# Ten instead of eight dummy products ahead of the first turn of the keys

## The chip, the cores and the metric

One core of one Trainium2 chip. The metric is the device time of one execution in microseconds (us), as a median over runs; lower is better. A profile gives the span of one execution; the device time of the same execution is 1.7 us longer (258.93 us for the profiled one of the kernel before, with a span of 257.2 us).

## The reference

Attention over 4 batches, 8 heads, 768 positions of 64, with a band of 16 positions and 24 block summaries, followed by a gated feed-forward layer on 3072 tokens of 512:

```python
k_sum = k.reshape(B, H, nb, block, D).max(axis=3)
v_sum = v.reshape(B, H, nb, block, D).mean(axis=3)
# scores on the band and on the block maxima, one softmax over both, then
x = attention_output                               # 3072 x 512
g = x @ w_gate; val = x @ w_val
ffn_out = gelu(g) * val @ w_out
return x + sigmoid(x @ w_res) * ffn_out
```

## The kernel before

The kernel works in eight units of 384 tokens. The parts that count here are its head, in which the first keys and queries are turned (transposed by TensorE), and the order in which weights are loaded. A "dummy" is a product of a tile of zeros with itself, whose result nobody reads.

```python
def keep_warm(n, wp=None):
    ...
    for i in range(n):
        nc.tensor.matmul(wp[:], warm[:, 0:128], warm[:], start=True, stop=True)

# loads on GpSimd's queue, in this order: keys, queries, values of the first unit (the keys and
# queries of its first two heads go on SyncE's queue), then
for c in range(6):
    sl = slice(c * 256, (c + 1) * 256)
    if c == 5:
        load_tokens(qb, q, 0, TU, S, 0, H)
    nc.gpsimd.dma_start(out=w_gate[:, :, sl], in_=wg_src[:, :, sl])
    nc.gpsimd.dma_start(out=w_val[:, :, sl], in_=wv_src[:, :, sl])
nc.gpsimd.dma_start(out=w_res[:], ...)
# ... w_out in three parts, then the next batch

# the head of TensorE's program
s1 = s_tiles((AO, TT))
keep_warm(8, s1[0])
nc.scalar.copy(kt[:, 0]..., kf[:, 0])              # cast of the first keys
nc.vector.tensor_copy(kt[:, 1]..., kf[:, 1])
nc.vector.tensor_copy(qa[:, 0:2]..., qf[:])
t = k_first(0)                                     # first turn of keys, 16 products
q_step(qa, 0, 0, TU, 0, *MM, nc.vector.tensor_copy)
keep_warm(2, s1[0])
# ... second turn, masks, dummies, first scores
```

The softmax here doesn't subtract the row's maximum and nothing guards it: scores larger than these inputs give would overflow.

Of the kernel before, what the change touches and what calls it, by code (L numbers as in the profile page):

```python
# [15 lines left out]
def kernel(  # L16
# [87 lines left out]
    with tc.manual_schedule():  # L104
# [200 lines left out]
        def s_tiles(two=None):  # L305
            if two:
                return [pool.tile([128, 512], F32, tag=tag, name="s1") for pool, tag in two]
            return ps_s.tile([128, 2, 512], F32, tag="s", name="s")
# [136 lines left out]
        def keep_warm(n, wp=None):  # L445
            if wp is None:
                wp = ps_mm.tile([128, 512], F32, tag="mm", name="wp")
            for i in range(n):
                nc.tensor.matmul(wp[:], warm[:, 0:128], warm[:], start=True, stop=True)  # L449
# [18 lines left out]
        st = new_unit()  # L468
        nc.scalar.activation(pre[:], bias_t[0:1, :], AF.Exp)
        s1 = s_tiles((AO, TT))  # L470
        keep_warm(8, s1[0])
        nc.scalar.copy(kt[:, 0].rearrange("p j d -> p (j d)"), kf[:, 0])
        nc.vector.tensor_copy(kt[:, 1].rearrange("p j d -> p (j d)"), kf[:, 1])
        nc.vector.tensor_copy(qa[:, 0:2].rearrange("p h j d -> p h (j d)"), qf[:])
# [245 lines left out]
```

## Time and profile before

| | before |
|---|---|
| device time, median of 3 runs | 257.66 us (257.52 to 258.19) |
| profiled execution: span | 257.2 us |
| TensorE busy | 250.6 us (97%) |
| TensorE's clock opens (clock record of the trace) | 10.63 us |
| first turn / first scores / first feed-forward product | 5.20 / 9.97 / 22.48 us |

The last rows are starts on TensorE's timeline. After 22.48 us TensorE never waits in this execution, so the last row counts most: what moves the first feed-forward product moves the end. The lines behind this are in the prediction.

### The profile page before, as it was taken

How to read it: one execution, taken by the hardware profiler on the slowest of the kernel's cores; microseconds unless marked ns; L12 is line 12 of the kernel's file. 1: busy time of each engine (PE TensorE's matmuls, PEld its weight loads, DVE VectorE, ACT ScalarE, POOL GpSimd, SP SyncE). 2: the span in 40 equal slices, each digit the busy share in tenths (PEclk: the TensorE clock that was granted, in tenths of full speed). 3: DMA queues.
4: the chain of work that ended last, by engine and by line, in shares of the span. 5: the costliest groups of instructions: out<-in, count | busy, mean ns of one | idle time of the engine just before them, and what ended most of it. 6: DMA issues, size and time to landing. Idle time of an engine off the chain costs nothing.

```text
span 257.2 us, 5751 instructions
## 1 busy us (share of the span) xinstructions
PE 250.6 (97%) x2240; PEld 139.8 (54%) x2240; DVE 172.6 (67%) x397; ACT 142.2 (55%) x249; POOL 103.5 (40%) x143
## 2 busy tenths in 40 slices
PE   7989999999999999999999999999999999999993
PEld 3445555566645555456654655556554655555543
DVE  4674975486487876779659768679568853764333
ACT  3584449645597536648683537458683537443310
POOL 7995533792979930028993560020001000010000
PEclk9999999999999999999999999999999999999999
DMA  7999999999999999759999999256003100130012
GB/s 152 157 144 195 197 204 201 149 172 150 128 152 172 168 149 159 109 136 148 162 129 151 183 154 131 49 143 120 0 3 88 82 3 1 33 138 3 0 41 83
DMA packets 118955, 30.46 MB, mean 118 GB/s; under 512 B 106064, under 2 KB 116752, under 8 KB 118928
## 3 DMA queue, kind: packets, MB, share of 16 engines
q0 software_dynamic: 86880, 19.90, 84.9%
q1 hardware_dynamic: 32048, 10.20, 25.2%
q8 instruction: 17, 0.28, 0.4%
q14 instruction: 10, 0.08, 0.1%
HBM read 32.51 MB, written 6.29 MB: 151 GB/s over the span
## 4 chain that ended last, share of the span: by engine, by line
PE 94%; ACT 2%; DMA 1%; DVE 1%; issue 0%; DVEq 0%
PE f L432 24%; PE vv L398 23%; PE g L398 22%; PE r L416 9%; PE gv L545 4%; PE ao L362 4%; PE s L330 3%; DMA kf<-in_k_dram 1%; PE xp L381 1%; PE vs L279 1%; PE s L449 1%; PE tp L226 1%; PE tp L195 1%; ACT kW L228 1%; PE gv L398 1%; PE tp L188 1%
## 5 line engine op out<-in xcount | busy, mean ns | idle before, releaser
L398 PE MATMUL vv<-xT,w_val 128*128 128x384 bf16 x360 | 73.7, 326 | 0.0
L404 ACT ACTIVATE ge<-g 128x384 f32<-128x384 f32 x85 | 41.8, 491 | 51.8 <-DVE gvT L405 25.9
L398 PE MATMUL g<-xT,w_gate 128*128 128x384 bf16 x340 | 69.7, 326 | 0.0
L405 DVE TENSOR_TENSOR gvT<-ge,vv 128x384 bf16<-128x384 f32 x90 | 49.2, 551 | 30.2 <-PE vv L398 26.9
L432 PE MATMUL f<-w_out,gvT 128*128 128x512 bf16 (+2 forms) x312 | 68.0, 363 | 0.0
L443 POOL DMA_DIRECT2D out_dram<-o x15 | 8.3, 552 | 100.4 <-DVE rz L370 81.9
L398 PEld LDWEIGHTS <-w_val 128*128 128x128 bf16 x364 | 35.6, 98 | 23.4
L398 PEld LDWEIGHTS <-w_gate 128*128 128x128 bf16 x344 | 33.3, 98 | 21.6
L432 PEld LDWEIGHTS <-gvT 128*128 128x128 bf16 x312 | 28.5, 98 | 28.9
L422 ACT ACTIVATE th<-r 128x512 f32<-128x512 f32 x24 | 14.2, 602 | 25.8 <-PE r L416 25.8
L437 DVE SCALAR_TENSOR_TENSOR th<-th,f 128x512 f32<-128x512 f32 (+2 forms) x26 | 16.7, 641 | 12.5 <-PE f L432 8.5
L416 PE MATMUL r<-w_res,xT 128*128 128x512 bf16 x96 | 24.4, 380 | 0.0
L175 POOL DMA_DIRECT2D k_sb<-in_k_dram x24 | 19.8, 836 | 11.2 <-DMA w_out<-in_moe_w_out_dram 5.2
L100 POOL DMA_DIRECT2D vext<-in_v_dram x28 | 23.6, 895 | 0.7 <-PE vv L398 0.7
L347 DVE TENSOR_TENSOR P<-P,maskt 128x768 bf16<-128x768 bf16 x28 | 15.5, 557 | 9.5 <-ACT P L336 5.0
L175 POOL DMA_DIRECT2D q_sb<-in_q_dram x24 | 19.8, 875 | 1.8 <-DMA k_sb<-in_k_dram 1.8
L372 DVE TENSOR_TENSOR xn<-ao,rz 128x384 bf16<-128x384 f32 x32 | 17.8, 557 | 1.1
L439 DVE SCALAR_TENSOR_TENSOR o<-th,xn 128x512 f32<-128x512 f32 (+2 forms) x26 | 16.9, 651 | 0.9
L336 ACT ACTIVATE P<-s,bias_t 128x384 bf16<-128x384 f32 x32 | 16.8, 578 | 1.1 <-PE s L330 1.1
L383 ACT COPY xT<-xp 128x384 bf16<-128x384 bf16 x17 | 7.9, 484 | 15.3 <-PE xp L381 15.3
L339 ACT ACTIVATE P<-s,bias_t 128x768 bf16<-128x768 f32 x16 | 14.5, 904 | 2.7 <-PE s L330 2.5
L175 POOL DMA_DIRECT2D v_sb<-in_v_dram x16 | 13.3, 925 | 0.0
(104 smaller groups left out, 248.9 us busy)
## 6 DMA issues: line engine op xcount, KB each, us to landing
out_dram<-o POOLq DMA_DIRECT2D x15, 256.0 KB, 2.4
vext<-in_v_dram POOLq DMA_DIRECT2D x20, 128.0 KB, 7.1
k_sb<-in_k_dram POOLq DMA_DIRECT2D x24, 96.0 KB, 7.8
q_sb<-in_q_dram POOLq DMA_DIRECT2D x24, 96.0 KB, 4.5
out_dram<-o SPq DMA_DIRECT2D x8, 256.0 KB, 3.8
w_gate<-in_moe_w_gate_dram POOLq DMA_DIRECT2D x6, 256.0 KB, 8.8
w_val<-in_moe_w_val_dram POOLq DMA_DIRECT2D x6, 256.0 KB, 9.1
w_out<-in_moe_w_out_dram POOLq DMA_DIRECT2D x3, 512.0 KB, 15.6
```

Of the source, the lines that this page charges most:

```text
L100: nc.gpsimd.dma_start(out=dst, in_=v[b, :, lo:hi, :].rearrange("h p d -> p h d"))
L175: nc.gpsimd.dma_start(out=sb[b][:, h // 2, :, h % 2 * D:h % 2 * D + D], in_=src[b, h].rearrange("(c p) d -> p c d", c=NC))
L336: nc.scalar.activation(P[:, hh].rearrange("p t q -> p (t q)"), s[hh][:, 0:TU], AF.Exp, scale=scale, bias=bias_t[:])
L347: nc.vector.tensor_mul(Pf, Pf, maskt.unsqueeze(1).to_broadcast([128, 2 * HT, QT]))
L372: nc.vector.tensor_mul(xn, ao[:, :, :, 0:D], rz.to_broadcast([128, NSUB, 2, D]))
L398: nc.tensor.matmul(acc[:, 0:TU], w[:, ko, fs], st["xT"][:, ko, :], start=(ko == 0), stop=(ko == KO - 1))
L404: nc.scalar.activation(ge[:], g[:, 0:TU], AF.Gelu)
L405: nc.vector.tensor_mul(gvT[:, fo, :], ge[:], vv[:, 0:TU])
L416: nc.tensor.matmul(r[:], st["xT"][:, ko, ss], w_res[:, ko, :], start=(ko == 0), stop=(ko == KO - 1))
L432: nc.tensor.matmul(st["f", sub][:, 0:c1 - c0], gvT[:, fo, ss], w_out[:, fo, c0:c1], start=(fo == 0), stop=(fo == FO - 1))
L437: nc.vector.scalar_tensor_tensor(th, th, 1.0, f[:, 0:c1 - c0], ALU.add, ALU.mult)
L439: nc.vector.scalar_tensor_tensor(o[:, 0:c1 - c0].rearrange("p (k d) -> p k d", d=128), th.rearrange("p (k d) -> p k d", d=128), 0.5, st["x ...
```

## The change

The intent: keys arrive some 4.5 us into the span and are cast until 5.2 us, but the eight dummies are over before that. Two more are to keep TensorE without a hole until the first turn, in the hope that its clock opens earlier than at 10.63 us.

```diff
         s1 = s_tiles((AO, TT))
-        keep_warm(8, s1[0])
+        keep_warm(10, s1[0])
```

## The prediction

The forecast's sum is 1.3 us of lead at the first feed-forward product, less 0.4 us for the last w_val: 257.66 - 0.9 = 256.8 us. The 1.3 us are worked out with the clock open at 7.21 us in place of 10.63. 7.21 us, and the range of 4.7 to 8.1 us for other executions, stand as assumptions.

> **What bounds the kernel now.** I read the page first, then the waits of TensorE over the whole span, then the chain of waits and the timeline of the first 45 us, and last the weight transfers. The engine line of the page:
>
> ```profile
> PE 250.6 (97%) x2240; PEld 139.8 (54%) x2240; DVE 172.6 (67%) x397; ACT 142.2 (55%) x249; POOL 103.5 (40%) x143
> ```
>
> TensorE is busy for 250.6 of 257.2 us. All it ever waits for, in the view of waits (us in total, times, longest):
>
> ```profile
> PE s L449 <- DVE warm L122: 1.3, 1, 1.3
> PE s L330 <- DVE kW L238: 0.7, 2, 0.5
> PE tp L226 <- ACT k L472: 0.3, 1, 0.3
> PE ao L362 <- DVE vsum L284: 0.2, 1, 0.2
> ```
>
> All four lie ahead of 21 us; after that TensorE runs without a wait until its last product, near 252 us. So whatever moves the moment at which the long run of products begins (22.5 us) moves the end by the same amount, unless a weight is late. The change touches only the first 6 us, which in the timeline (start, us, engine, line, operation) hold:
>
> ```profile
> 1.27 3.60 PE L449 MATMUL s<-warm 128*128 128x512 bf16 x8 [1.27 <-DVE warm L122]
> ...
> 4.53 0.62 ACT L472 CAST k<-kf 96x512 bf16<-96x512 f32 x1 [2.21 <-DMA kf<-in_k_dram]
> ...
> 5.20 0.85 PE L226 MATMUL tp<-ident,k 96*64 96x96 bf16 x16 [0.33 <-ACT k L472]
> ```
>
> Eight dummies run while the first keys fly in. The last is over at 4.87 us, the cast of the keys ends at 5.15 us, and the first turn starts at 5.20 us. Between them TensorE is empty for 0.33 us by the view; by the pitch of the dummies (0.427 us each, eight end their streaming at 1.27 + 3.41 = 4.69 us) nearer 0.5 us. From there the chain of waits is TensorE alone:
>
> ```profile
> 5.20 0.85 PE tp L226 x16
> 6.05 0.32 PE tp L195 x8
> 6.37 0.96 PE s L449 x2
> 7.33 0.78 PE tp L226 x15
> 8.11 0.32 PE tp L195 x8
> 8.43 0.75 PE s L313 x2
> 9.18 0.85 PE s L449 x2
> 10.04 0.43 PE s L330 x12
> 10.47 0.63 PE s L449 x2
> ```
>
> What to see: two dummies cost 0.85 us here and two mask products 0.75 us, while later the same things go in half: two mask products at 12.27 us take 0.50 us with their drain, and the sixteen turns at 11.36 us take 0.53 instead of 0.85 us. All of 5.2 to 10.6 us is the critical path, and all of it is at half speed. The page's clock row shows nine tenths in every slice and misses this; the raw clock record of the trace holds one stretch at full clock that opens 10.63 us after the start of the span and lasts 245.76 us.
>
> [...]
>
> **The change part by part.** It removes and moves nothing on VectorE, ScalarE, GpSimd and the DMA queues; TensorE gets two more weight loads and two more 128x512 products at its head, and only buffer names differ after that.
>
> *Cost.* Ten dummies stream until 1.27 + 10 x 0.427 = 5.54 us. The first turn then starts at about 5.6 us (a gap of about 0.1 us follows dummies ahead of a turn, as after the pair at 6.3 us), 0.4 us later than now. If nothing else changed, the first turn, the following two dummies and the second turn would move back by that. The keys of the second turn landed at 6.8 us (issued 1.40, 5.4 to landing) and are no limit. If the clock still opened at 10.63 us, 0.4 us of cold work would be pushed behind it and run there in half, so about 0.2 us would arrive at the end, or less where ScalarE's copies take over from 11.9 us.
>
> *Gain.* The hole closes: from 1.27 us on TensorE is dense. [...]so the clock opens at 7.21[...]. Then, with warm durations from after 11.3 us of this trace:
> - second turn and its queries from about 7.4 to 8.05 us (0.36 + 0.27 by start-to-start, against 0.65 + 0.45 cold), two masks and two dummies to 8.8 us;
> - the first scores wait for VectorE's copies of the first window: ScalarE's copy ends at about 7.3, the block maximum 0.95 and copies some 0.7 us more give 9.0 us, against 10.0 now;
> - their exponential on ScalarE goes at about 9.45 instead of 10.58; third turn at 10.0 instead of 11.36, its ScalarE copy at 10.6 instead of 11.93; from there the chain is ScalarE (copy, copy, exponential, copy), VectorE (maximum, copies), scores, all of unchanged length. So the fourth scores start at about 14.95 instead of 16.30 us and the long run at 21.1 to 21.2 instead of 22.5.
> That is 1.3 us at 22 us.
>
> *What is not kept.* The weights come at the pace of the DMA engines[...]; the window table shows 195 to 205 GB/s from 22 to 40 us, and GpSimd's issues there wait for earlier transfers. The tightest is the last chunk of w_val (issue, then time to landing, then first use):
>
> ```profile
> 24.67 0.74 POOL L161 DMA_DIRECT2D w_val<-in_moe_w_val_dram  x1 [1.31 <-DMA w_gate<-in_moe_w_gate_dram]
> ```
> ```profile
> w_val<-in_moe_w_val_dram POOLq DMA_DIRECT2D x1, 256.0 KB, 11.5
> ```
> ```profile
> 37.11 0.81 PE L398 MATMUL vv<-xT,w_val 128*128 128x384 bf16 x4
> ```
>
> It lands at 24.67 + 11.5 = 36.2 us and is used at 37.11: slack 0.9 us. The other chunks have 1.7 to 5 us of slack (w_res lands at 38.5, used 40.18; first w_out at 41.1, used 42.78; last w_gate at 33.9, used 36.45). So of 1.3 us gained, about 0.4 us turn into a new wait of TensorE for w_val near 36 us, and 0.9 us reach the end: 257.66 - 0.9 = 256.8 us, or 0.3%.
>
> **The rivals.**
> 1. *The clock does not open earlier*[...]. Time: 257.66 + 0.1 to 0.3, about 257.9 us. I give it 20%.
> 2. *The clock opens earlier, but the ScalarE and VectorE chain swallows it.* For it: from 11.9 to 16.3 us these two, not TensorE, carry the chain. Against it: that chain starts from a turn on TensorE and a copy, and moves with it. If it swallowed half of it: 257.0 us.
> 3. *The weights give no limit*, because landings move or the slack is larger than read: the whole 1.3 us, 256.3 us. Against it: nothing in the change makes transfers start sooner.
> 4. [...]runs of both kernels scatter over up to 1 us and the medians differ by chance. The means should still differ by about 0.8 us, since VectorE and w_val also clip what an earlier opening can give.
>
> **Range and chances.** Weighted: 0.75 to 0.8 for 256.3 to 257.0 us, the rest around 257.9. I take 256.8 us, 8 times in 10 between 256.3 and 257.8. Two dummies at 0.43 us[...] cannot reach 2% (5.2 us) either way: within 2% 0.98, 0.01 on each side.
>
> **What would show it.** Right: ten dummies until about 5.7 us; no hole ahead of the first turn, which starts near 5.6 us; the full clock and half-length products from about 7.2 us, or from any point between 4.7 and 8.1, instead of 10.6; first scores near 9.0 us; a new wait of TensorE for the last w_val near 36 us of some 0.4 us. Wrong: products of 0.43 us pitch still at 9 us (the clock step fails); a start of the long run no earlier than 22.3 us (rival 2); no wait at w_val and an end 1.3 us earlier (rival 3).

## The result, and the profile after

The median of ten dummies was 257.71 us (257.36 to 258.11, 4 runs), of before 257.63 us in the same rounds; the ratio is 0.9999 (95% interval 0.9976 to 1.0023). Ratios here are the mean time of one kernel's fast runs over that of the other's fast runs of the same rounds, so not quite the ratio of the medians that are quoted. The time did not move, although in the profiled pair the span fell from 257.2 to 256.4 us.

The head did what it should. Timeline of the kernel after (start, us, engine, line, operation):

```profile
1.27 4.28 PE L449 MATMUL s<-warm 128*128 128x512 bf16 x10 [1.27 <-DVE warm L122]
...
5.48 0.53 PE L226 MATMUL tp<-ident,k 96*64 96x96 bf16 x16
```

The first turn has no idle time in brackets any more, and its sixteen products take 0.53 us where they took 0.85: the clock is open already. The clock record has it open at 5.26 us, in place of 10.63. First scores start at 8.81 us (9.97 before). The first feed-forward product, kernel before, then kernel after, each from its timeline:

```profile
22.48 0.32 PE L398 MATMUL gv<-xT,w_gate 128*128 128x384 bf16 x1
```
```profile
20.94 0.32 PE L398 MATMUL gv<-xT,w_gate 128*128 128x384 bf16 x1
```

That is 1.54 us earlier. Then the view of TensorE's waits of the kernel after shows what before had not (some lines):

```profile
PE gv L545 <- DMA xT<-xn: 0.4, 1, 0.4
PE vv L398 <- DMA w_val<-in_moe_w_val_dram: 0.2, 1, 0.2
```

and the timeline, the place of the second one:

```profile
35.97 0.82 PE L398 MATMUL vv<-xT,w_val 128*128 128x384 bf16 x4 [0.23 <-DMA w_val<-in_moe_w_val_dram]
```

This product started at 37.11 us before: 1.14 us are left of 1.54. The lead stays at 1.1 to 1.3 us until 141 us, where the wait for a transposing transfer takes 0.5 us of it; 0.8 us reach the end. So the profiled pair agrees with the prediction, and the timed runs do not. The profiled execution of before, 258.93 us, was slower than every timed run of before in those rounds (257.52 to 258.19).

### The profile page after: what moved, and what is told of

Read it like the earlier page. It is cut to its first block, busy times and chain, and to the rows that moved or that the text cites. A ratio compares the mean times of both kernels' runs of the same rounds, so it can differ in the third digit from the quotient of the medians.

```text
span 256.4 us, 5729 instructions
## 1 busy us (share of the span) xinstructions
PE 247.4 (96%) x2216; PEld 138.7 (54%) x2242; DVE 172.4 (67%) x397; ACT 142.1 (55%) x249; POOL 103.8 (40%) x143
## 4 chain that ended last, share of the span: by engine, by line
PE 80%; DMA 10%; POOL 5%; issue 1%; ACT 1%; DVE 1%; POOLq 0%; DVEq 0%
PE f L432 22%; PE vv L398 21%; PE g L398 19%; PE r L416 8%; DMA w_val<-in_moe_w_val_dram 5%; PE gv L545 4%; DMA w_gate<-in_moe_w_gate_dram 3%; PE ao L362 3%; PE s L330 2%; DMA xT<-xn 2%; POOL vext L100 2%; POOL k L91 1%; PE xp L381 1%; POOL qa L91 1%; PE vs L279 1%
## 5 line engine op out<-in xcount | busy, mean ns | idle before, releaser
L432 PE MATMUL f<-w_out,gvT 128*128 128x512 bf16 (+2 forms) x298 | 66.0, 362 | 0.8 <-issue 0.2
```

The costliest lines, as they stand in the source:

```text
L432: nc.tensor.matmul(st["f", sub][:, 0:c1 - c0], gvT[:, fo, ss], w_out[:, fo, c0:c1], start=(fo == 0), stop=(fo == FO - 1))
```

## The experiments

Twelve runs were made, in three jobs of four, each with six runs beside eleven of before on the same chip. Two theories were on trial. A: the moment at which the clock opens differs from one execution of a kernel to the next, and the profiled one of before (10.63 us) was a late draw. B: the landing of the last weights cuts off what an early clock gives.

**How the closing of the clock is read in a run without a profile.** In the clock records of the fourteen profiled executions the stretch at full clock lasts 245.76, 249.17 or 252.59 us; in before and b8, where it opened late, it lasts 245.76 us. Behind it the record has half clock (0.5 in before and after), and only this end is in the mean clock of a run: before, with 0.99837 in the trace over 257.2 us, has by that 0.84 us at half clock, and its record closes 0.84 us ahead of the end. So (1 - mean clock) x 2 x span is the time that a run spent at half clock at its end, and the span less this is the moment at which the clock closed. It is an estimate, good to about 0.26 us because the mean clock is given to three decimals; a run with mean clock 1.000 cannot be read. And it chooses its runs: where the clock would close behind the end of a run, nothing is seen. In before and b8 it closed 256.38 and 256.32 us after the start; in s10b, s10, a10 and d14 at 256.6 to 257.3 us, behind the end of their spans (255.2 to 257.0 us). So a closing later than about 256.1 us can be read only in a run that is late anyhow. It is the same near 255.8 us: of s8 and s8b below, which closed at 255.81 and 255.77 us, only the late one has a mean clock below 1.000.

**Repeats of both kernels: b8, a10, a10b, a10c.** No edit.

> The kernel before once more, for its scatter and for a second profile. Theory A ([...]the profiled execution of before, 257.2 us of span with the clock opening at 10.63 us, was a late draw): the opening in this profile lies anywhere between 4.7 and 11 us, and the span is below 256.6 us if the opening is earlier than 9 us. Theory B (the last weights set the start of the undisturbed run, so an earlier clock is cut off there): whatever the opening, the span stays within 255.6 to 256.6 us once it is earlier than about 9.5 us. Time against before: ratio 1.000, inside 0.997 to 1.003.

> The changed kernel once more (ten dummies). Theory A: opening between 4.7 and 8.2 us in every profile, mean time 0.3 to 0.8 us below before once enough runs are averaged (ratio 0.997 to 0.999). Theory B: ratio 1.000 within 0.001, with a wait of TensorE for the last w_val of 0.1 to 0.5 us in the profile.

> The changed kernel once more, for numbers: ten dummies against before in the same rounds. Theory A and B together (ten dummies take away only the late draws of before, 258.4 us and above, and leave the others where the weights hold them): ratio 0.997 to 0.999, no run of ten dummies above 258.3 us, one third of the runs of before above it. If the two kernels are simply the same: ratio 0.9995 to 1.0005, and as many slow runs in one as in the other.

> Ten dummies a last time, for numbers. So far, pooled over all rounds: before 32 runs, median 257.77, mean 258.01, 8 runs above 258.3 us; ten dummies 16 runs, median 257.74, mean 257.73, 1 run above 258.3. If the change only takes away late draws of the clock: the medians stay within 0.15 us of each other, about a quarter of the runs of before and at most one of six with ten dummies lie above 258.3 us, mean 0.2 to 0.4 us lower. If the two are simply the same: as many slow runs in both.

Measured against before in the same rounds: b8 1.0018 (0.9978 to 1.0058), a10 0.9983 (0.9959 to 1.0007), a10b 1.0008 (0.9988 to 1.0028), a10c 0.9999 (0.9977 to 1.0022). Pooled with the first result:

| | runs | median | mean (standard error) | spread (s.d.) | above 258.3 us |
|---|---|---|---|---|---|
| eight dummies | 43 | 257.85 | 258.07 (0.10) | 0.67 | 14 |
| ten dummies | 22 | 257.84 | 257.84 (0.10) | 0.48 | 3 |

Medians alike; the mean differs by 0.24 us with a standard error of 0.14, so it is not clear of zero. One run of eight, 260.64 us in b8 (mean clock 1.000, cause unknown), makes 0.06 us of it, and ten against before in the same rounds alone gives 0.13 us. The slow runs are fewer. The bet of a10b that no run of ten lies above 258.3 us was lost (258.58), and a10c had two (258.71, 259.07). The closing can be read in 28 unprofiled or profiled runs of eight (one more, of mean clock 0.993, is left out: it has 3.6 us at half clock where the others have 2.1 us at most, which hardly come from the end alone) and in 14 of ten:

| clock closed at | eight: runs, mean, range | ten: runs, mean, range |
|---|---|---|
| 256.15 to 256.59 us | 6, 258.89, 258.69 to 259.40 | none |
| 253.75 to 255.77 us | 22, 257.80, 257.13 to 258.67 | 14, 257.69, 257.21 to 258.11 |

That all six runs of eight that closed at 256.15 to 256.59 us are slow, at 258.9 us, is no finding by itself, since a fast one could not be read there. They are counted as late draws because the two profiles that closed there opened late; of runs without a profile the opening is not on record. But a slow one would be read in either kernel: there are six among the 39 runs of eight whose mean clock is on record, and none among the 22 of ten. Were the kernels alike, that would come by chance about once in 17 times; so that ten dummies take away these late draws is likely, and not shown. The two profiles of the kernel before that exist (before and b8: open at 10.63 and 10.56 us, spans 257.2 and 257.0 us) both closed there. Without the six, the other 37 runs of eight have a mean of 257.94 us (257.86 without the one of 260.64), and ten dummies 257.84. This is theory A, and it says where the predicted gain is: in the late draws only. No profile caught the kernel before with an early opening; that most of its runs have one is inferred from their times, from d0, and from s8 below, which has the same head and opened at 6.63 us.

Late draws are not the only slow runs. The four above 258.3 us among the 22 closed at 254.75 to 255.77 us. s8b below, which closed at 255.77 us, opened at 10.01 us, and s8, which closed at 255.81 us, at 6.63 us, so there a late opening is possible and not certain. The three slow runs of ten all had mean clock 1.000 and no profile; with spans of 256.9 to 257.4 us a closing at 256.15 to 256.59 us would have shown, so their cause is another, and open. Late transfers can be one: in the profile of s10 the clock was open at 4.41 us, and it still took 258.03 us, with waits of 0.8 us in all for values ahead of the feed-forward (which began at 21.72 us) and of 0.4 us for xT.

In a10's profile the clock opened at 4.49 us and the feed-forward began at 20.25 us, 2.23 us earlier than in before. Its timeline near 35 us:

```profile
34.53 0.82 PE L398 MATMUL g<-xT,w_gate 128*128 128x384 bf16 x4 [0.24 <-DMA w_gate<-in_moe_w_gate_dram]
35.86 0.82 PE L398 MATMUL vv<-xT,w_val 128*128 128x384 bf16 x4 [0.51 <-DMA w_val<-in_moe_w_val_dram]
```

Of 2.23 us, 1.25 are left at this product. That is theory B: an opening at 4.49 us and one at 5.26 us meet at the same weights (35.86 and 35.97 us).

**d0: no dummies.**

```diff
-        keep_warm(8, s1[0])
+        keep_warm(0, s1[0])
```

> No dummies at all ahead of the first turn (0 in place of 8); the result stays right. TensorE starts at 5.2 us[...]. If an early clock is worth anything at the end of the kernel, this is slower than before: theory A 0.2 to 0.8 us (ratio 1.001 to 1.003). Theory B: the same as before within 0.2 us (ratio 1.000 to 1.001), since the weights land when they land. A third theory C (the dummies ahead of the first turn cost more than they give) has it faster than before.

Measured: 259.08 us median (258.56 to 259.27), ratio 1.0033 (1.0009 to 1.0058); the clock opened at 9.35 us. Its mean, 258.98 us, is that of the late draws of eight (258.89), 1.0 us above the 37 other runs of eight and 1.3 us above ten dummies in the same rounds (a10, 257.67). So the early clock is worth 1.0 to 1.3 us, and eight dummies already earn it in most executions. The bet of C falls, and that of B (no change) too, though the interval reaches down to it.

**d14: six dummies more.**

```diff
-        keep_warm(8, s1[0])
+        keep_warm(14, s1[0])
```

> Fourteen dummies ahead of the first turn, six more than before. With the clock opening between 4.7 and 7.2 us they end at 6.3 to 7.2 us, so the first turn starts 1.1 to 2.0 us later than in before, but then runs at full speed. Theory A: first scores near 9.8 to 10.5 us, about where they are in a late draw of before: ratio 1.000 to 1.003. Theory B: the delay is hidden behind the landing of the last w_val as long as it is below about 1 us: ratio 1.000 to 1.002. If neither holds and the delay is paid in full: 0.8 us and more, ratio over 1.003.

Measured: 258.65 us median (257.75 to 258.72), ratio 1.0011 (0.9985 to 1.0037): no difference from before clear of noise. Against ten dummies in the same rounds (a10: mean 257.67 us, standard error 0.10) its mean of 258.40 (0.17) is 0.7 us slower: dummies beyond the arrival of the keys cost time. The profile had the clock open at 4.73, the first turn at 6.08 and the feed-forward at 21.33 us, and still a wait of 0.5 us for w_val, which landed later than in other profiles (its product started at 36.67 us). So transfers scatter from one execution to the next, too: in a10b the same product started at 35.59 us without waiting, 1.1 us earlier.

**x10: w_res ahead of the last chunk.** With ten dummies.

```diff
                 load_tokens(qb, q, 0, TU, S, 0, H)
+                nc.gpsimd.dma_start(out=w_res[:], in_=moe_w_res.rearrange("(ko ki) f -> ki ko f", ki=128))
             nc.gpsimd.dma_start(out=w_gate[:, :, sl], in_=wg_src[:, :, sl])
             nc.gpsimd.dma_start(out=w_val[:, :, sl], in_=wv_src[:, :, sl])
-        nc.gpsimd.dma_start(out=w_res[:], in_=moe_w_res.rearrange("(ko ki) f -> ki ko f", ki=128))
```

> Ten dummies, and w_res (512 KB) loaded ahead of the last chunk of w_gate and w_val in place of behind it; nothing else moves. The last w_val then lands 512 KB / 0.196 MB/us = 2.7 us later, at about 38.6 us. Theory B: TensorE waits for it 2.5 to 3.5 us and the whole delay beyond the present wait arrives at the end: 2.2 to 2.8 us slower than ten dummies, about 260.2 us, ratio to before 1.008 to 1.011. If weights are not the limit: unchanged, ratio 0.998.

Measured: 261.94 us median (259.72 to 263.77), ratio 1.0142 (1.0101 to 1.0184), worse than bet. Timeline of its profile (259.73 us):

```profile
36.81 0.82 PE L398 MATMUL g<-xT,w_gate 128*128 128x384 bf16 x4 [1.36 <-DMA w_gate<-in_moe_w_gate_dram]
38.10 0.82 PE L398 MATMUL vv<-xT,w_val 128*128 128x384 bf16 x4 [0.47 <-DMA w_val<-in_moe_w_val_dram]
```

The product on the last w_val moved from 35.86 (a10) to 38.10 us, that is by 2.24 us, and this execution took 259.73 us where the profiled one of a10 had taken 257.53: a later weight is paid whole, which is theory B. The other four runs of x10, 261.6 to 263.8 us (one of them, 263.77, slow), had mean clocks of 0.983 to 0.993, which is 3.6 to 8.9 us at half clock. They have no profile, so where in them the clock was at half, and why, is not shown; in the profiled one, with waits of 1.36 and 0.47 us, the mean clock is 1.000.

**s8, s10, s9: the last chunk in halves.** With eight, ten and nine dummies; s8 and s10 ran twice (s8b, s10b).

```diff
-            nc.gpsimd.dma_start(out=w_gate[:, :, sl], in_=wg_src[:, :, sl])
-            nc.gpsimd.dma_start(out=w_val[:, :, sl], in_=wv_src[:, :, sl])
+            for s in ((sl,) if c < 5 else (slice(1280, 1408), slice(1408, 1536))):
+                nc.gpsimd.dma_start(out=w_gate[:, :, s], in_=wg_src[:, :, s])
+                nc.gpsimd.dma_start(out=w_val[:, :, s], in_=wv_src[:, :, s])
```

> Ten dummies, and the last chunk of w_gate and w_val loaded as two halves of 128 columns, in the order gate, val, gate, val, so that the half that is needed first lands about 1.3 us earlier (half of two transfers of 256 KB at the 0.196 MB/us that the window table of before shows). Theory B (the landing of the last weights cuts off what an early clock gives): the wait for w_val near 36 us goes or shrinks below 0.2 us, the first product on the last chunk starts at 34.9 to 35.6 us in place of 35.9 to 36.0, and the time falls by 0.3 to 0.7 us under that of ten dummies alone, to about 257.0 us (ratio to before 0.996 to 0.9975), unless the next transfers (w_res, w_out) take over as the limit at once, which would show as waits for them. Theory A alone[...]: the same as ten dummies, ratio 0.998.

> The same split of the last chunk with eight dummies. Theory B: in early draws of the clock 0.2 to 0.4 us faster than before, in late draws (opening after 9.5 us) no change, because there the weights already wait for TensorE; ratio 0.998 to 1.000, and slower than the split with ten dummies by 0.3 to 0.8 us in the mean. Theory A alone: ratio 1.000.

> The split of the last weights with eight dummies once more. Weights as the limit: ratio to before 0.997 to 0.9985 as in its first job (0.9974), with one or two late draws near 257.8 to 258.5 us in six if the clock's late draws are real[...]. No late draw at all in twelve runs would speak against a quarter of late draws.

> The split with ten dummies once more. If the early clock is worth something once the weights no longer cut it off: equal to or faster than the split with eight, by 0 to 0.4 us in the mean, no run above 258 us. If the two extra dummies cost what they delay, 0.2 to 0.4 us slower than the split with eight, as in the first job (257.30 against 256.92 us).

> The split with nine dummies: they end streaming at 1.27 + 9 x 0.427 = 5.11 us, before the first turn can start (4.9 to 5.2 us) or at most 0.2 us after, so the hole closes and the turn is hardly held up. If both the hole and the delay count: as fast as the faster of eight and ten or faster, 256.7 to 257.1 us, no late draws. In the profile the clock opens before 8.2 us and the first turn starts no later than 5.3 us.

Measured, ratio to before in the same rounds, and mean of all runs:

| | dummies | ratios | runs, mean |
|---|---|---|---|
| s8, s8b | 8 | 0.9974 (0.9957 to 0.9992), 0.9953 (0.9931 to 0.9974) | 12, 256.99 us |
| s10, s10b | 10 | 0.9983 (0.9966 to 1.0001), 0.9959 (0.9940 to 0.9977) | 12, 257.26 us |
| s9 | 9 | 0.9964 (0.9945 to 0.9983) | 6, 257.35 us |

All three are faster than before, by 0.2 to 0.5% (the interval of s10 reaches 1.0001), and than ten dummies in the same rounds, by 0.5 to 1.1 us. No wait for w_val or w_gate is left in the five profiles; in that of s8 the next transfer in line has taken its place, as the bet allowed:

```profile
PE r L417 <- DMA w_res<-in_moe_w_res_dram: 0.4, 1, 0.4
```

But the profiles do not show the gain there. TensorE's last product ends at 251.89, 251.56, 251.68 and 252.45 us with ten dummies alone (a10, a10b, a10c, after), and at 251.79, 251.73, 251.72 and 252.84 us with the split and an early clock (s8, s10b, s9, s10): no earlier. What is shorter is the end of the program behind it. From the end of the last product to the end of the span it takes 3.95 to 3.99 us in all nine profiles without the split, and 3.46 to 3.48 us in all five with it. From a10b, then s10b: the span, the last operation of VectorE in the timeline, and a wait of the closing lines from the view of SyncE's waits:

```profile
core 0 of [0], span 255.5 us
251.96 0.29 DVE L439 SCALAR_TENSOR_TENSOR o<-th,xn 128x128 f32<-128x128 f32 x1
SPq L715 <- PEq L715: 1.1, 2, 0.9
```
```profile
core 0 of [0], span 255.2 us
252.14 0.29 DVE L440 SCALAR_TENSOR_TENSOR o<-th,xn 128x128 f32<-128x128 f32 x1
SPq L716 <- PEq L716: 0.7, 2, 0.5
```

These 0.5 us are a large part, in s10 all, of the 0.4 to 1.2 us by which the means of the split lie under before in the same rounds, in a place where no weight is loaded; the late draw has them as well (s8b took 257.88 us, before 258.93 and b8 258.69). Why the program closes sooner is open. So the split is faster, but it does not show that the weights were the limit; the waits in after, a10 and d14 and the delay in x10 do.

Whether eight, ten or nine dummies go best with the split is not settled: in the one job that ran all three the means are 257.06, 257.22 and 257.35 us, with standard errors of 0.24, 0.16 and 0.17. The bet of s8 that ten would be faster by 0.3 to 0.8 us is lost, and so are that of s9 (256.7 to 257.1 us, no late draw; one run took 258.06) and the ratio that s10 bet (0.996 to 0.9975).

The two profiles of the split with eight dummies are the cleanest evidence on the hole. Their clocks closed within 0.04 us of each other (255.81 and 255.77 us), the keys landed 0.3 us apart. s8, then s8b, timelines:

```profile
1.27 3.60 PE L450 MATMUL s<-warm 128*128 128x512 bf16 x8 [1.27 <-DVE warm L122]
4.90 0.85 PE L227 MATMUL tp<-ident,k 96*64 96x96 bf16 x16
...
6.83 0.53 PE L227 MATMUL tp<-ident,k 96*64 96x96 bf16 x16
```
```profile
1.27 3.60 PE L450 MATMUL s<-warm 128*128 128x512 bf16 x8 [1.27 <-DVE warm L122]
5.24 0.85 PE L227 MATMUL tp<-ident,k 96*64 96x96 bf16 x16 [0.38 <-ACT k L473]
...
7.31 0.85 PE L227 MATMUL tp<-ident,k 96*64 96x96 bf16 x16
```

In s8 the keys came early and the hole, by the pitch of the dummies, is 4.90 - 4.69 = 0.2 us; the clock opened at 6.63 us, and the second turn takes 0.53 us. In s8b the hole is 0.55 us; the clock opened at 10.01 us, 3.38 us later, and the second turn still takes 0.85 us. Device times 256.95 and 257.88 us. And s9, whose nine dummies end at 5.11 us, with the turn at 5.28 us, opened at 6.52 us.

**The hole and the opening.** From all profiles with eight, nine or no dummies (end of the dummies by their pitch of 0.427 us):

| profile | dummies end, us | first turn, us | hole, us | clock opened, us |
|---|---|---|---|---|
| before | 4.69 | 5.20 | 0.51 | 10.63 |
| b8 | 4.69 | 5.21 | 0.52 | 10.56 |
| s8b | 4.69 | 5.24 | 0.55 | 10.01 |
| s8 | 4.69 | 4.90 | 0.21 | 6.63 |
| s9 | 5.11 | 5.28 | 0.17 | 6.52 |
| d0 | none | 5.41 | | 9.35 |

The three with a hole of 0.5 us opened at 10.0 to 10.6 us, the two with a hole of 0.2 us at 6.5 and 6.6 us. These are one execution each, and d0, in which TensorE did nothing before 5.41 us, opened ahead of the three. So the profiles show that a small hole went with an early opening here; what in TensorE's work opens the clock they do not show.

## Why the prediction was right or wrong

- *The hole closes, the clock opens earlier, the feed-forward starts near 21.1 us:* right in the profile of after (5.26 us, 20.94 us), and in the three repeats (4.49 to 6.18 us; 20.25 to 21.03 us).
- *Cost of the two dummies 0.4 us at the first turn:* it starts at 5.48 us in the profile of after and at 5.61 and 5.65 us in those of a10b and a10c, against 5.20 us before: 0.3 to 0.45 us later. In a10, where the clock opened ahead of the last dummies, it starts at 5.18 us and costs nothing.
- *The last w_val takes about 0.4 us back:* the mechanism is right, the wait was 0.2 us in after and 0.5 us in a10, and none in a10b and a10c, where the weights came sooner. x10 shows that the landing is a real limit. A wait that was not foreseen, for a transposed xT near 141 us, took another 0.5 us in the profile of after.
- *257.66 - 0.9 = 256.8 us:* this step failed. The 0.9 us were the gain over the profiled execution of before and were subtracted from the median of the timed ones. The profile was a late draw (258.93 us); the timed runs were mostly early ones that had little to gain. Late draws (clock closed at 256.15 to 256.59 us) are six of 39 runs of eight dummies, and 1.0 us is at stake there (258.89 against 257.94): 0.15 us in the mean, the size of the 0.13 to 0.24 us found (not clear of zero), and nothing in the median. The page's own times had the warning: the profiled execution was above all three timed runs. That the measured 257.71 us still lies in the stated range (256.3 to 257.8) is owed to the room that it left for no gain, and not to the mechanism, which had 75 to 80% of the weight.
- *The clock opens at 7.21 us in place of 10.63:* this hid the mistake. The author took it that ten dummies open the clock that much earlier than eight in nearly every execution; that was an estimate from one profile. With the same eight dummies s8 opened at 6.63 us, and the times of before say that most of its executions do not open late. Measured with ten dummies were 5.26 us in after and 4.49 to 6.18 us in the repeats. The gain can also be larger than predicted: in a10 the clock opened 6.1 us earlier than in before, and the feed-forward began 2.23 us earlier.
- *Rival 4, runs of both kernels scatter over up to 1 us and the medians differ by chance,* was nearest to what happened; its added claim that the means differ by 0.8 us was not. *Rival 1* is refuted by the profiles; that its 257.9 us came close has another reason. *Rival 3* is refuted by after and a10, but in a10b and a10c it held: no wait for a weight, and spans 1.7 and 1.6 us shorter than that of before. *Rival 2* did not happen: of the opening's head start 1.54 us arrived at the feed-forward, more than the 1.3 us predicted.

## What to carry to other kernels

Before a gain is worked out from a profile, compare the profiled execution's own time with the timed runs: where something differs between executions of one kernel, as the opening of TensorE's clock did here (4.49 to 6.18 us in four profiles with ten dummies, 6.63 and 10.01 us in the two of the split with eight), one profile is one draw, and what is gained over a bad draw does not come off the median. A little early speed is worth only as much as the slack of the transfers behind it: of 2.23 us gained ahead of the feed-forward in a10, 1.25 us were left at the last w_val. When an edit makes a kernel faster, look through the whole trace for the place where the time went: half a microsecond of what the split of a weight gave lies behind the last product. Dummies ahead of the first work should reach to the moment when its data is usually ready, and no further: here fourteen were 0.7 us slower than ten.
